# A linear-attention block and a multiplicative FFN on one core: the last 882 of 1382 steps in another order

## The chip, the cores and the metric

The kernel runs on one core of a Trainium2 chip. The metric is the device time of one execution in microseconds. Of the kernel before there are three runs, 556.48, 558.15 and 558.35 us, with a median of 558.15.

The engines are named as in the profile: PE (TensorE's matmuls), PEld (its weight loads), DVE (VectorE), ACT (ScalarE), POOL (GpSimd) and SP (SyncE, which issues the DMAs here).

## The reference

```python
# deltanet, q k v: (4, 8, 768, 48), beta: (4, 8, 768)
k_n = k / (np.linalg.norm(k, axis=-1, keepdims=True) + 1e-06)
for t in range(S):
    y[:, :, t] = np.einsum('bhd,bhde->bhe', q[:, :, t], state)
    v_old = np.einsum('bhde,bhd->bhe', state, kt)
    state = state + bt[:, :, :, None] * np.einsum('bhd,bhe->bhde', kt, vt - v_old)
# bridge: (B,H,S,D) -> (B*S, H*D), x is 3072 x 384
# ffn, w1 w2: (384, 1024), w3: (1024, 1024), w_out: (1024, 384)
a = x @ w1
b = x @ w2
h = a * b @ w3
return (h @ w_out).astype(np.float32)
```

All values are float32.

## The kernel before

**The attention.** The 768 positions are cut into 12 chunks of 64, two of which make a pair. Within a chunk the recurrence is solved in closed form: a triangular matrix U of scaled key scores is inverted, and the state passes from chunk to chunk. For one chunk m, the steps and their lines are these.

- d: the keys and queries are transposed on DVE into KQ (L355).
- s: the scores, in two halves. PE writes one PSUM buffer of the pool "ps_w" (L451, L457), DVE makes U (L463) and the masked query scores PT (L474) out of it. The pool has two buffers, used in turn by everything that writes ps_w.
- u and V: U of a pair goes out to DRAM and comes back in blocks of 32 (DMAs Ud<-U L491, Ub<-Ud L510). DVE inverts the blocks in place, 31 pairs of operations on Vb (L524, L529). Then Vb goes out (L549) and comes back as T and TT.
- e: the corner between the blocks, with two bursts of small matmuls (L619) and a copy on ACT behind each (L635, L646).
- c: the chain. PE multiplies S and KQ (L672), DVE makes the right-hand side R (L706), PE multiplies R and TT, DVE makes X (L717), PE multiplies X and the keys, and DVE makes the next state S (L738). Each needs the one ahead of it.
- y: the outputs (L777), which are three bursts on PE, first KQ and S, then PT and X, then KQ and S again. ACT copies them into xT (L795), and DMAs move some strips of xT (L806).
- g, N and n are the keys' norms (POOL's squares L301, DVE's sums L303, small DVE operations L310 to L334) and the scaling of v on POOL (L658). k, v and p are loads.

**The FFN.** Behind a pair u stand the FFN's 256 positions of each batch pair. The step a makes ab = (x w1) * (x w2) in eight pieces: PE (L934), a copy by ACT (L946), PE again (L934), and DVE's multiply out of PSUM (L950). S is sums of these pieces on POOL (L1007). o multiplies by the folded w3 w_out in seven products of 16 matmuls (L1166, a fast matrix multiplication with seven products instead of eight). x adds the products up on DVE and ACT (L1197, L1201, L1203) and stores them (L1182). PE's results of the FFN lie in the pool "ps_f" with four banks, used in turn. The last pair has another form of a (L1074) with sums made on POOL (X and W, L1026 to L1052).

**The order.** Each step is a piece of a generator. ORDER (L39 to L87) is a string of 1382 step names, and each name advances one generator by one piece. A name whose generator has ended does nothing. At the end every engine's instructions are bound to the order in which they were written:

```python
    for name in ORDER.split():
        step(name)
    in_text_order()
```

So ORDER sets the order on each engine, and an engine that waits for one instruction holds up all that stand behind it. It also sets which buffer of a pool a step gets, since pools are used in turn. The text overlaps three things: while the blocks of one pair are inverted on DVE, PE runs the products a of an earlier pair, and in between PE mixes the products o with the short bursts of s, e, c and y.

## Time and profile before

| what | us |
|---|---|
| median of three runs | 558.15 |
| lowest, highest | 556.48, 558.35 |
| span of the profiled execution | 556.1 |
| PE busy in it | 533.6 |
| DVE busy | 343.7 |
| ACT busy | 145.7 |
| POOL busy | 169.7 |

The profiled execution's own time is not listed apart from its span. The median of the runs lies 2.05 us above that span. In the rows that the prediction quotes, times are microseconds, the first number of a timeline row is its start within the span, the second its duration, and brackets hold the idle time of that engine just before, with what ended it. The steps that are moved begin at about 152 us.

### The profile page before, as it was taken

How to read it: one execution, taken by the hardware profiler on the slowest of the kernel's cores; microseconds unless marked ns; L12 is line 12 of the kernel's file. 1: busy time of each engine (PE TensorE's matmuls, PEld its weight loads, DVE VectorE, ACT ScalarE, POOL GpSimd, SP SyncE). 2: the span in 40 equal slices, each digit the busy share in tenths (PEclk: the TensorE clock that was granted, in tenths of full speed). 3: DMA queues.
4: the chain of work that ended last, by engine and by line, in shares of the span. 5: the costliest groups of instructions: out<-in, count | busy, mean ns of one | idle time of the engine just before them, and what ended most of it. 6: DMA issues, size and time to landing. Idle time of an engine off the chain costs nothing.

```text
span 556.1 us, 19932 instructions
## 1 busy us (share of the span) xinstructions
PE 533.6 (96%) x8732; PEld 390.8 (70%) x8732; DVE 343.7 (62%) x800; ACT 145.7 (26%) x291; POOL 169.7 (31%) x213
## 2 busy tenths in 40 slices
PE   6699999999999999999999999999999999989997
PEld 5556667788998544888444897445995447988897
DVE  6799738589546498574995354885373973213552
ACT  2786567531121120220111211202201102212200
POOL 7574443527730002812102522004540027420000
PEclk9999999999999999999999999999999999999999
DMA  9999956594423593453745453605307222020001
GB/s 189 339 307 230 158 140 150 128 160 55 96 48 55 119 147 72 67 88 89 122 74 100 70 91 80 126 38 83 51 15 154 26 60 38 18 58 1 0 2 57
DMA packets 191527, 54.22 MB, mean 98 GB/s; under 512 B 178928, under 2 KB 185072, under 8 KB 191440
## 3 DMA queue, kind: packets, MB, share of 16 engines
q1 hardware_dynamic: 189328, 52.56, 46.3%
q8 instruction: 68, 1.11, 0.9%
q10 hardware_dynamic: 2112, 0.39, 0.5%
q14 instruction: 19, 0.16, 0.1%
HBM read 41.78 MB, written 9.96 MB: 93 GB/s over the span
## 4 chain that ended last, share of the span: by engine, by line
PE 93%; DVE 3%; issue 2%; DMA 2%; ACT 0%; SPq 0%; DVEq 0%
PE ps_f L934 38%; PE ps_f L1166 20%; PE ps_f L913 7%; PE ps_w L672 6%; PE ps_w L777 4%; PE ps_f L1074 4%; PE ps_w L619 3%; PE ps_w L1074 2%; PE ps_w L451 2%; PE ps_f L369 1%; PE ps_w L457 1%; PE ps_f L904 1%; DMA beta_fm<-in_beta_dram 1%; PE ps_w L409 1%; PE ps_w L1166 1%
## 5 line engine op out<-in xcount | busy, mean ns | idle before, releaser
L934 PE MATMUL ps_f<-xT,w2s 128*128 128x512 f32 (+1 forms) x288 | 106.9, 524 | 0.0
L934 PE MATMUL ps_f<-xT,w1s 128*128 128x512 f32 (+1 forms) x288 | 106.7, 524 | 0.0
L934 PEld LDWEIGHTS ps_f<-xT,w2s 128*128 128x128 f32 x288 | 54.1, 190 | 46.5 <-issue 41.6
L934 PEld LDWEIGHTS ps_f<-xT,w1s 128*128 128x128 f32 x288 | 54.0, 190 | 45.3 <-issue 41.6
L1007 POOL TENSOR_TENSOR ab<-ab 128x256 f32<-128x256 f32 x80 | 56.4, 731 | 78.7 <-DVE ab L950 73.8
L946 ACT COPY ab<-ps_f 128x512 f32<-128x512 f32 (+1 forms) x48 | 24.3, 515 | 134.4 <-PE ps_f L934 130.3
L1166 PE MATMUL ps_f<-w,ab 128*128 128x192 f32 x320 | 57.3, 332 | 1.9 <-DVE osb L1197 1.3
L1166 PEld LDWEIGHTS ps_f<-w,ab 128*128 128x128 f32 x320 | 51.6, 190 | 3.3 <-issue 2.4
L524 DVE TENSOR_TENSOR tb<-Vb,Ub 128x31 f32<-128x31 f32 (+15 forms) x124 | 43.0, 347 | 15.4 <-DMA Ub<-Ud 11.5
L529 DVE TENSOR_TENSOR Vb<-Vb,tb 128x31 f32<-128x31 f32 (+15 forms) x124 | 43.0, 346 | 4.3
L913 PE MATMUL ps_f<-wo,w3T 128*128 128x384 f32 x128 | 43.5, 491 | 0.4 <-ACT w3T L907 0.4
L1166 PE MATMUL ps_f<-room,ab 128*128 128x192 f32 x240 | 42.8, 332 | 0.0
L950 DVE TENSOR_TENSOR ab<-ab,ps_f 128x512 f32<-128x512 f32 (+1 forms) x48 | 27.4, 589 | 24.0 <-PE ps_f L934 24.0
L1166 PEld LDWEIGHTS ps_f<-room,ab 128*128 128x128 f32 x240 | 38.7, 190 | 0.7
L913 PEld LDWEIGHTS ps_f<-wo,w3T 128*128 128x128 f32 x128 | 23.5, 190 | 15.4 <-ACT w3T L907 0.5
L301 POOL TENSOR_TENSOR sq<-ktok 128x384 f32<-128x384 f32 x24 | 19.7, 835 | 43.5 <-DMA out_dram<-osb 16.9
L658 POOL TENSOR_TENSOR vtok<-vtok,n 128x384 f32<-128x384 f32 x24 | 19.8, 832 | 39.5 <-DMA vtok<-in_v_dram 39.5
L635 ACT COPY T<-ps_w 32x512 f32<-32x512 f32 x24 | 13.8, 577 | 67.2 <-PE ps_w L619 46.2
L795 ACT COPY xT<-ps_w 112x256 f32<-112x256 f32 x48 | 14.3, 384 | 65.0 <-PE ps_w L777 61.7
L451 PE MATMUL ps_w<-KQ 48*64 48x128 f32 x320 | 21.9, 274 | 1.8 <-DVE PT L474 1.5
L717 DVE TENSOR_TENSOR X<-ps_w,wt 128x768 f32<-128x768 f32 x12 | 11.5, 956 | 19.4 <-PE ps_w L672 12.9
L1197 DVE TENSOR_TENSOR room<-room,ps_f 128x384 f32<-128x384 f32 (+1 forms) x13 | 7.0, 537 | 26.4 <-PE ps_f L1166 26.4
(170 smaller groups left out, 805.9 us busy)
## 6 DMA issues: line engine op xcount, KB each, us to landing
vtok<-in_v_dram SPq DMA_DIRECT2D x24, 192.0 KB, 4.4
out_dram<-osb SPq DMA_DIRECT2D x23, 192.0 KB, 2.6
ktok<-in_k_dram SPq DMA_DIRECT2D x44, 96.0 KB, 3.4
raw<-in_moe_w_dram SPq DMA_DIRECT2D x8, 512.0 KB, 6.2
raw<-in_moe_w_dram SPq DMA_DIRECT2D x18, 192.0 KB, 4.5
raw<-in_moe_w_out_dram SPq DMA_DIRECT2D x7, 384.0 KB, 5.3
Ud<-U SPq DMA_DIRECT2D x40, 64.0 KB, 2.8
Ub<-Ud SPq DMA_DIRECT2D x5, 512.0 KB, 4.2
```

The costliest lines, as they stand in the source:

```text
L451: pe.matmul(ps[half(z), 0, n : n + 128], lhsT=x[:, 0, :], rhs=x.rearrange("p j t -> p (j t)"), start=True, stop=True,)
L524: dve.tensor_tensor(out=tv, in0=V[:, 0 : s + 1, s : s + 1].to_broadcast([P, s + 1, n]), in1=U[:, s, s + 1 : BS].unsqueeze(1).to_broadcast( ...
L529: dve.tensor_tensor(out=o, in0=o, in1=tv, op=ALU.subtract)
L672: pe.matmul(out(ps, r, h, z), lhsT=lhs(r, h, z), rhs=rhs(r, h, z), start=True, stop=True,)
L777: i = pe.matmul(region(h, z, r), lhsT=lhs, rhs=rhs, start=part[n] not in part[:n], stop=part[n] not in part[n + 1 :],)
L913: pe.matmul(ps[:, 0:DM], lhsT=w3Ts[jc, kc // 4][:, kc % 4 * P : kc % 4 * P + P], rhs=wo(kc), start=(kc == 0), stop=(kc == KF - 1),)
L934: pe.matmul(ps[:].rearrange("p b c t -> p b (c t)"), lhsT=w[:, m, js], rhs=x[:, m, :, c0:c1].rearrange("p b c t -> p b (c t)"), start=(m = ...
L946: act.copy(out=t, in_=ps)
L950: dve.tensor_tensor(out=t, in0=t, in1=ps, op=ALU.mult)
L1007: (dve if u == last else pool).tensor_tensor(out=o_, in0=x_, in1=y_, op=op)
L1074: pe.matmul(ps[:, j, :], lhsT=w[j], rhs=x, start=first and j == 0, stop=j == 1, skip_group_check=not first,)
L1166: pe.matmul(ps[b][:, b, :], lhsT=ab_of(u, HF * f + i, t0), rhs=ws_[w][:, i], start=first and i == 0 and (b == 0 or n == "F"), stop=i == HF ...
```

## The change

ORDER is replaced. The first 500 names are the same, the other 882 are the same names in another order, and nothing is added or removed. One more line is needed for the string, so every line number behind it is higher by one in the changed kernel. The words with the change say that VectorE's SBUF-only operations are kept off GpSimd's. The core of the diff is one line of the table before, and the one in which the same steps stand now:

```diff
-o0 x0 y3 s4 s4 d5 d5 s4 s4 N2 s5 y3 u4 s5 V2 s5 s5 s5 N2 s5 c3 u5 V2 x0 p6 x0 a14 p6 a14 a14 a14
...
+c3 c3 S0 o0 S0 S0 S0 S0 x0 x0 x0 c3 c3 y3 y3 d5 d5 s4 s4 s4 s4 d5 d5 y3 s4 s4 s5 s5 s5 u4 s5 s5
```

The following rows show three places. The first is the run of chunks 3 to 5, ahead of the first inversion that is moved. PE's order there, before, from the chain of chunk 3 to the scores of chunk 4 ("R,TT" is the chain's multiplication, "room" and "w" are weights of the products o):

```order
L672 MATMUL ps_w<-R,TT_89 64x48 x32
L1166 MATMUL ps_f<-room,ab 128x192 x8
L777 MATMUL ps_w<-KQ,S 48x64 x16
L777 MATMUL ps_w<-PT,X 48x64 x32
L777 MATMUL ps_w<-KQ,S 48x64 x16
L451 MATMUL ps_w<-KQ 64x128 x2
```

And PE's order there in the changed kernel:

```order
L673 MATMUL ps_w<-R,TT_89 64x48 x32
L778 MATMUL ps_w<-KQ,S 48x64 x16
L778 MATMUL ps_w<-PT,X 48x64 x32
L778 MATMUL ps_w<-KQ,S 48x64 x16
L452 MATMUL ps_w<-KQ 64x128 x2
```

The product o has left its place between the chain and the outputs; a second one that stood between the two halves of chunk 4's scores has also gone to a place behind the scores. On DVE, the same run, before, from chunk 3's X on (kperm and qperm are the keys and queries to be transposed, osb a result to be stored; the numbers tell buffers apart, and PT_2765 and PT_2836 are chunks 4 and 5):

```order
L717 TENSOR_TENSOR X_2652<-ps_w_103,wt_1514 128x2x8x48
L1197 TENSOR_TENSOR room_2013<-room_2013,ps_f_95 128x384
L1197 TENSOR_TENSOR osb_2720<-room_2013,ps_f_93 128x384
L355 STREAM_TRANSPOSE KQ_2723<-kperm_91 128x8x64 x2
L463 TENSOR_TENSOR U_106<-ps_w_103,wt_2528 128x512
L1197 TENSOR_TENSOR osb_2759<-room_2013,ps_f_97 128x384
L474 TENSOR_TENSOR PT_2765<-ps_w_103,smask_86 128x512
L355 STREAM_TRANSPOSE KQ_2723<-qperm_92 128x8x64 x2
L463 TENSOR_TENSOR U_106<-ps_w_101,wt_2528 128x512
L474 TENSOR_TENSOR PT_2765<-ps_w_101,smask_86 128x512
```

The same in the changed kernel, where PT_2758 and PT_2819 are chunks 4 and 5:

```order
L718 TENSOR_TENSOR X_2659<-ps_w_103,wt_1514 128x2x8x48
L356 STREAM_TRANSPOSE KQ_2730<-kperm_91 128x8x64 x2
L464 TENSOR_TENSOR U_106<-ps_w_103,wt_2413 128x512
L475 TENSOR_TENSOR PT_2758<-ps_w_103,smask_86 128x512
L356 STREAM_TRANSPOSE KQ_2730<-qperm_92 128x8x64 x2
L464 TENSOR_TENSOR U_106<-ps_w_101,wt_2413 128x512
L475 TENSOR_TENSOR PT_2758<-ps_w_101,smask_86 128x512
```

DVE's own list is the same but for the additions to osb, which have moved away; chunk 5's query transposes still stand behind chunk 4's first U and PT.

The second place is the end of the mixed part. PE's order before, from the chain of chunk 11 to the last stage's first features (L1074):

```order
L672 MATMUL ps_w<-R,TT_89 64x48 x32
L1166 MATMUL ps_f<-room,ab 128x192 x8
L777 MATMUL ps_w<-KQ,S 48x64 x16
L777 MATMUL ps_w<-PT,X 48x64 x32
L777 MATMUL ps_w<-KQ,S 48x64 x16
L1166 MATMUL ps_f<-room,ab 128x192 x8
L1166 MATMUL ps_f<-w_117,ab 128x192 x8
L1074 MATMUL ps_f<-xT,w1s 128x256 x6
```

And in the changed kernel:

```order
L673 MATMUL ps_w<-R,TT_89 64x48 x32
L778 MATMUL ps_w<-KQ,S 48x64 x16
L778 MATMUL ps_w<-PT,X 48x64 x32
L778 MATMUL ps_w<-KQ,S 48x64 x16
L1167 MATMUL ps_f<-room,ab 128x192 x16
L1075 MATMUL ps_f<-xT,w1s 128x256 x2
L1167 MATMUL ps_f<-w_117,ab 128x192 x8
```

Here too the product between chain and outputs has gone behind the outputs, and two features of the last stage now stand ahead of the last product of the pair before.

The third place is the first moved inversion. DVE's order before, at its end:

```order
L524 TENSOR_TENSOR tb_3062<-Vb_2833,Ub_2902 128x31
L529 TENSOR_TENSOR Vb_2833<-Vb_2833,tb_3062 128x31
L950 TENSOR_TENSOR ab_2992<-ab_2992,ps_f_93 128x512
L355 STREAM_TRANSPOSE KQ_3081<-kperm_91 128x8x64 x2
L355 STREAM_TRANSPOSE KQ_3081<-qperm_92 128x8x64
L950 TENSOR_TENSOR ab_3074<-ab_3074,ps_f_95 128x512
```

In the changed kernel, inside the inversion, behind 22 of its 31 pairs:

```order
L525 TENSOR_TENSOR tb_3006<-Vb_2237,Ub_2896 128x220
L530 TENSOR_TENSOR Vb_2237<-Vb_2237,tb_3006 128x22x10
L951 TENSOR_TENSOR ab_2989<-ab_2989,ps_f_97 128x512
L525 TENSOR_TENSOR tb_3018<-Vb_2237,Ub_2896 128x207
L530 TENSOR_TENSOR Vb_2237<-Vb_2237,tb_3018 128x23x9
```

Before, the stage's first multiply stands ahead of the 31 pairs and the second behind them all. Now the first stands behind 22 pairs, and the rest behind all of them.

## The prediction

> **What bounds the kernel now.** I read the page first: the busy shares, then the chain that ended last.

> ```profile
> PE 533.6 (96%) x8732; PEld 390.8 (70%) x8732; DVE 343.7 (62%) x800; ACT 145.7 (26%) x291; POOL 169.7 (31%) x213
> PE 93%; DVE 3%; issue 2%; DMA 2%; ACT 0%; SPq 0%; DVEq 0%
> ```

> TensorE (PE) is busy 96% of the span and 93% of the last chain. VectorE (DVE) is 3% of that chain. A reordering that removes no work can therefore win only idle time of PE, or lose by adding some. The second view is the busy time by stretch, cut where the stages change. Its columns are the stretch, its length, busy time and instructions of PE, PEld, DVE, ACT and POOL, the granted clock, the DMA share and GB/s.

> ```profile
> 152.00:265.00 113.00, 109.64 (x2408) 80.66 (x2408) 72.81 (x173) 18.97 (x41) 25.04 (x36) 1.00 0.48 86
> 265.00:303.00 38.00, 38.00 (x216) 17.60 (x211) 30.60 (x76) 4.70 (x9) 4.91 (x6) 1.00 0.58 98
> 342.00:381.00 39.00, 39.00 (x266) 18.20 (x256) 29.35 (x77) 4.80 (x9) 3.12 (x5) 1.00 0.43 91
> ```

> The kernel alternates. In 265 to 303 and 342 to 381, where DVE inverts the triangular blocks and PE runs the first two products of the FFN, PE is busy all of the time. In the stretches between, where scores, state and outputs go back and forth between PE and DVE, it idles a little. The clock is 1.00 in every row, so no term comes from it. The third view sums what PE waited for from 152 us on, which is where the changed steps begin. Its columns are the total, the number of waits and the longest.

> ```profile
> PE ps_f L1166 <- DVE osb L1197: 1.3, 1, 1.3
> PE ps_w L451 <- DVE PT L474: 1.0, 3, 0.5
> PE ps_w L672 <- issue: 0.8, 2, 0.5
> PE ps_w L672 <- DVE X L717: 0.5, 1, 0.5
> PE ps_f L1166 <- DVE tb L524: 0.5, 1, 0.5
> PE ps_w L672 <- DVE PT L474: 0.2, 1, 0.2
> ```

> That is 4.3 us, of which 0.8 us ("issue") waits for nothing that the order names. So 3.5 us in seven waits is what an order could remove.

> **What the change removes.** The lengths of single waits come from PE's timeline: start, duration, what ran, and in brackets the idle time before it.

> ```profile
> 156.43 0.77 PE L619 MATMUL ps_w<-T,U 33*33 33x32 f32 x64
> 157.69 0.94 PE L672 MATMUL ps_w<-X,ktok 64*48 64x48 f32 x64 [0.49 <-DVE X L717]
> 162.32 0.77 PE L619 MATMUL ps_w<-T,T 33*33 33x32 f32 x64
> 163.01 2.87 PE L1166 MATMUL ps_f<-room,ab 128*128 128x192 f32 x16
> ```

> A burst of 64 corner matmuls hands over to the next 0.69 us after its start (162.32 to 163.01). At 156.43 the next burst started 1.26 us after, so the wait cost 0.57 us against the 0.49 that stands as idle, because the modelled end of a burst overlaps its successor. With 0.08 us more for each, the seven waits are worth 3.5 + 7 x 0.08 = 4.1 us. In the new order each of their places is arranged otherwise, and I count all of it as removed.

> The change also leaves fewer entries into the large matmuls. Counted in PE's order from the first changed row on, there are 40 uninterrupted runs of large matmuls before and 36 after.

> ```profile
> 152.73 2.80 PE ps_f L1166 x16
> 534.35 13.00 PE ps_f L1166 x80
> ```

> In the chain, 16 such matmuls entered from small ones take 2.80 us, and in a run of 80 they take 13.00 / 5 = 2.60 us. An entry costs 0.2 us, and four fewer give 0.8 us.

> **What the name of the change says.** It keeps DVE's operations on SBUF away from GpSimd's (POOL). The trace shows what that is worth:

> ```profile
> 269.88 0.40 DVE L524 TENSOR_TENSOR tb<-Vb,Ub 128x231 f32<-128x231 f32 x1
> 270.01 0.95 POOL L301 TENSOR_TENSOR sq<-ktok 128x384 f32<-128x384 f32 x1 [16.94 <-DMA out_dram<-osb]
> 270.31 0.90 DVE L529 TENSOR_TENSOR Vb<-Vb,tb 128x231 f32<-128x231 f32 x1
> 274.40 0.42 DVE L529 TENSOR_TENSOR Vb<-Vb,tb 128x255 f32<-128x255 f32 x1
> 274.84 0.83 POOL L301 TENSOR_TENSOR sq<-ktok 128x384 f32<-128x384 f32 x1 [3.88 <-DVE Vb L529]
> 274.86 1.09 DVE L524 TENSOR_TENSOR tb<-Vb,Ub 128x256 f32<-128x256 f32 x1
> ```

> Beside a POOL square the two DVE operations take 0.90 and 1.09 us where their neighbours take 0.40 and 0.42, so 0.50 + 0.67 = 1.2 us are lost. Both lie inside 265 to 303, where PE is busy 38.00 of 38.00 us. DVE has slack there (30.60 of 38.00), so the loss reaches nobody. I put this relief at 0. Its bounds are 0 and 1.2 us.

> [...]

> **What the change adds.** In each mixed stretch I read the new order of PE and DVE row by row, asking how much PE work stands between a burst and the DVE result that the following one needs. The prices come from these rows:

> ```profile
> 156.68 0.96 DVE L717 TENSOR_TENSOR X<-ps_w,wt 128x768 f32<-128x768 f32 x1 [2.48 <-PE ps_w L672]
> 174.71 0.27 PE L451 MATMUL ps_w<-KQ 48*64 48x128 f32 x1
> 174.95 1.19 ACT L795 COPY xT<-ps_w 112x256 f32<-112x256 f32 x4 [5.54 <-PE ps_w L777]
> 175.75 2.87 PE L1166 MATMUL ps_f<-w,ab 128*128 128x192 f32 x16
> 175.88 0.69 DVE L463 TENSOR_TENSOR U<-ps_w,wt 128x512 f32<-128x512 f32 x1 [0.86 <-PE ps_w L457]
> 180.45 0.68 DVE L474 TENSOR_TENSOR PT<-ps_w,smask 128x512 f32<-128x512 f32 x1
> 177.55 1.29 DVE L355 STREAM_TRANSPOSE KQ<-qperm 128x512 f32<-128x512 f32 x2
> 486.99 0.67 PE L777 MATMUL ps_w<-KQ,S 48*48 48x64 f32 x32
> 487.47 1.08 PE L777 MATMUL ps_w<-PT,X 64*48 64x64 f32 x64
> ```

> *Chunks 3 to 5 (near 165 to 182 us).* Before, a product of 2.80 us stands between R,TT and the outputs, and hides X. Now the outputs follow R,TT directly. X is ready 1.26 us after the point where PE could go on (the row at 157.69), and KQ,S covers 0.48 (486.99 to 487.47): 0.8 us of wait. Chunk 4's second half of the scores now follows its first half directly. It needs the bank that ACT empties at 174.95 + 1.19 = 176.14, while the first half ends at 175.75: 0.4 us. Chunk 5's scores need the query transposes. These now stand on DVE behind U and PT: 0.13 (175.75 to 175.88) + 0.6 + 0.6 + 1.29 = 2.6 us after the first half. The 0.4 us wait and the second half itself (1.0 us, as 174.71 to 175.75) cover 1.4 of that, so 1.2 us are left. Two smaller waits behind PT follow in the same run, 0.2 us each. Together 2.8 us, of which the first 0.8 is as good as certain.

> *Chunks 5 to 7.* Half a score burst's bank is free about 1.5 us after its burst (0.13 + 0.6 + 0.68, and a start), and a state burst covers 1.0 of it. This stands twice: 0.5 + 0.5. A tenth comes from c5's short chain. The last product of the pair still follows the one that DVE's x1 must free a bank for, as before at 0.5 us. Together 1.6 us.

> *Chunks 9 and 10.* S,KQ to R,TT needs 1.26 us, and half a score burst of about 1.0 lies between: 0.3. The next half waits for PT behind R: 0.6. Together 0.9 us.

> *Chunks 10 and 11 (the end).* Chunk 11 has the same R,TT, KQ,S, PT,X as above: 0.8. The corner's copy on ACT stands between e10 and c10: 0.5. Then the first matmuls of the last stage stand ahead of the last product, and need the xT transfers:

> ```profile
> 490.61 3.74 SPq L806 DMA_DIRECT2D xT<-xT  x6
> 495.90 2.34 POOL L1052 TENSOR_TENSOR xT<-xT 128x256 f32<-128x256 f32 x3 [16.81 <-DMA xT<-xT]
> ```

> The transfers are issued until 494.35, and POOL reads xT at 495.90. Two products after the outputs end about 494.7. The wait is between 0 and 1.2 us, and I take 0.3, since the first matmuls need only the earlier strips. It replaces the 1.3 us for osb in the waits above. Together 1.6 us.

> **The sum.** 2.8 + 1.6 + 0.9 + 1.6 = 6.9 us added, 4.1 + 0.8 = 4.9 removed: 2.0 us more. The profiled span is 556.1 us, and the median of the runs, 558.15, lies 2.05 above it, which I leave as it is. So 556.1 + 2.0 + 2.05 = 560.2 us. If 3 us of the unsure waits are covered, 3.9 us are added, and the time is 557.2. If each of ten waits is 0.3 us longer than its row, it is 563.2.

> **The inversions.** The four later inversions hold the rest of the change. There PE now does more of the w1 products first, and DVE's multiplies stand elsewhere among the inversion's steps.

> ```profile
> 181.09 5.49 SPq L491 DMA_DIRECT2D Ud<-U  x8
> 188.13 0.34 SPq L510 DMA_DIRECT2D Ub<-Ud  x1
> 188.52 0.95 SPq L1182 DMA_DIRECT2D out_dram<-osb  x1
> 192.96 0.19 DVE L524 TENSOR_TENSOR tb<-Vb,Ub 128x31 f32<-128x31 f32 x1 [3.51 <-DMA Ub<-Ud]
> 216.21 0.68 DVE L950 TENSOR_TENSOR ab<-ab,ps_f 128x512 f32<-128x512 f32 x1
> 183.31 39.05 PE ps_f L934 x90
> ```

> A product of six matmuls takes 39.05 / 15 = 2.6 us, and an inversion takes 23.3 us (192.96 to 216.21). Counting products until the first bank that must be freed by DVE, I find at least 0 to 0.7 us of slack in the second inversion, 0.3 in the fourth, 2.3 in the first, and more in the third. On SP's queue, a store and two loads of v now stand between Ud and Ub in the first one: 0.95 + 2 x 0.6 (5.49 / 8 each) = 2.2 us of issue, of which the 1.55 us gap (186.58 to 188.13) hides most. 0.6 us later costs nothing against 2.3. I put the inversions at 0.

> **The rivals.** *Covered waits.* The bursts on PE arrive later than I count, and DVE and ACT are earlier. Then only what is removed counts, with the certain 0.8 twice: 558.15 - 4.9 + 1.6 = 554.9. For it speaks that most of DVE's and ACT's work in these stretches is short. Against it, the rows at 156.68 and 175.88 start at once behind PE, so DVE is not late and cannot become earlier. If the 1.2 us of the two long rows came off as well, it would be 553.7.

> *The banks.* An inversion that starts late keeps the multiplies queued behind its steps, and PE's product waits for a bank. It decides from 0.3 us late in the fourth and 0.7 in the second. If Ub lands 3 us later in each, which nearly doubles the 3.51 us that DVE waits for it at 192.96, PE loses 0.7 + 2.6 + 2.7 = 6 us on top: about 566, slower than before by more than 1%. For it speaks the number of transfers now between Ud and Ub; against it, PE's row of 38.00 in 38.00.

> *The change does nothing.* The loss that it names is 1.2 us off PE's path, and added and removed waits cancel: 558.2.

> **Chances.** The forecast, 557 to 563, has 0.60; covered waits 0.15; the banks 0.17; nothing 0.08. The measurement of this kernel can tell about 0.5%, or 2.8 us. Faster by more than that (under 555.4) is two thirds of the covered waits: 0.10. Slower (over 560.9) is the banks and a third of the forecast: 0.37. The same is left with 0.53. The range is 555.5 to 564.0: it leaves out most of the first rival's gain and the upper half of the second's.

> **What would show it.** Right: in the waits after, DVE's X ahead of PT,X (L778) twice at 0.7 to 0.9 us; KQ's transposes (L356) ahead of L452 at about 1.2; the 1.3 us osb wait gone; PE's sum of idle from 152 us on at 6 to 8 us; the stretch of each inversion still full. Whether inversion steps still take 0.9 us beside POOL changes nothing. Wrong: idle under 4 us in all, or a wait of L935 for DVE's multiply (L951).

## The result and the profile after

| | us |
|---|---|
| before, median of 6 runs | 557.76 (556.48 to 558.53) |
| after, median of 6 runs | 565.13 (561.47 to 567.03) |
| after, the profiled execution | 566.52, span 564.8 |

The ratio after to before is 1.0132, with an interval of 1.0108 to 1.0156. The changed kernel is 7.4 us slower. The prediction said 560.2, with a range from 555.5 to 564.0, and the measured time lies 1.1 us above the range. Its sign is right, and its size is 4.9 us too small. A second set of the same kernel on another chip had a median of 563.36 (run 10 below). The ratios come with a 95% interval and are not quotients of the medians shown; one execution, the slowest of s2's four, is left out of them.

The page of the kernel after shows the engines' busy time and the last chain.

```profile
PE 535.5 (95%) x8732; PEld 392.2 (69%) x8732; DVE 347.4 (62%) x800; ACT 145.9 (26%) x291; POOL 169.3 (30%) x213
PE 73%; DVE 13%; DMA 5%; issue 4%; SPq 4%; ACT 1%; POOL 0%; ACTq 0%; DVEq 0%; POOLq 0%
```

PE has the same 8732 matmuls and 1.9 us more busy time. What grew most is its idle time, from 22.5 to 29.3 us of the span. The chain has changed more than the time did: it now leaves PE for an inversion on DVE, for DMA and for SP. The stretches that the prediction quoted read as follows.

```profile
152.00:265.00 113.00, 108.23 (x2327) 78.94 (x2314) 72.13 (x168) 18.89 (x41) 23.01 (x33) 1.00 0.47 83
265.00:303.00 38.00, 38.00 (x157) 17.75 (x156) 28.96 (x70) 5.85 (x10) 3.95 (x5) 1.00 0.68 116
342.00:381.00 39.00, 39.00 (x221) 18.74 (x220) 27.86 (x74) 4.50 (x8) 2.53 (x4) 1.00 0.60 116
```

The inversions still lie under a full PE, 38.00 of 38.00 and 39.00 of 39.00 us. The mixed stretch has 1.4 us more idle time. PE's largest waits from 152 us on, and two smaller ones that the prediction named, are these.

```profile
PE ps_w L620 <- DVE T L603: 2.3, 1, 2.3
PE ps_w L778 <- DVE X L718: 1.4, 2, 0.7
PE ps_w L673 <- issue: 1.1, 2, 0.9
PE ps_w L778 <- issue: 1.0, 2, 0.7
PE ps_f L1167 <- DVE room L1198: 0.7, 1, 0.7
...
PE ps_w L452 <- ACT xT L796: 0.4, 1, 0.4
...
PE ps_w L452 <- DVE KQ L356: 0.2, 1, 0.2
```

X stands twice at 0.7, as predicted. KQ is 0.2 where 1.2 was expected. At the head stands a wait that no step of the prediction has: the corner's burst L620 waits 2.3 us for T. Two "issue" rows, 2.1 us together, wait for nothing that the order names. Before, there were 0.8 us of these. All waits from 152 us on add up to 10.3 us, where the prediction had named 6 to 8 as a sign of being right. The 1.3 us wait for osb is gone. A wait of L935 for L951, which it had named as a sign of being wrong, is there with 0.3 us.

**Where it went.** To keep the modelled ends out of the sum, I measure from the start of each matmul to the start of the next and take off the usual distance of that shape. Of what is left from 152 us on, gaps over 0.16 us are single waits, and the rest is entries into large matmuls and rounding.

| from 152 us on | before | after |
|---|---|---|
| single gaps over 0.16 us | 10.1 | 18.4 |
| of these, stalls inside bursts ("issue") | 1.2 | 3.0 |
| of these, the corner that waits for T | 0 | 2.5 |
| slower matmuls in 3.4 us of half clock | 0 | 1.7 |
| the small rest | 21.9 | 21.2 |

Added up, the kernel after has 18.4 - 10.1 + 1.7 - 0.7 = 9.3 us more, against 8.7 us between the spans. Three entries have no term in the prediction: packets of instructions 1.8, the corner 2.5, the clock 1.7, in all 6.0 us. The waits that it did sum make up the other 3.3, where it had 2.0. All of this is one execution of each kernel.

**The corner.** SP's timeline of the kernel before, around the inversion of chunks 8 and 9:

```profile
345.30 0.34 SPq L510 DMA_DIRECT2D Ub<-Ud  x1
372.12 0.35 SPq L549 DMA_DIRECT2D Vd<-Vb  x1
374.81 1.91 SPq L583 DMA_DIRECT2D TT<-Vd  x4
...
378.78 2.05 SPq L583 DMA_DIRECT2D TT<-Vd  x4
```

The same of the kernel after:

```profile
347.23 0.53 SPq L511 DMA_DIRECT2D Ub<-Ud  x1
378.00 0.36 SPq L550 DMA_DIRECT2D Vd<-Vb  x1
382.99 1.91 SPq L584 DMA_DIRECT2D TT<-Vd  x4
...
387.00 4.96 SPq L262 DMA_DIRECT2D qperm<-in_q_dram  x8
392.01 2.12 SPq L584 DMA_DIRECT2D TT<-Vd  x4
```

The first row is 1.9 us later, and from there to Vd it takes 30.8 us instead of 26.8: DVE starts on Ub 5.67 instead of 3.44 us after its issue, and the steps, with more of DVE's other work among them, take 25.1 instead of 23.3 us. From Vd to the first TT it takes 5.0 instead of 2.7 us. Then the loads of a later chunk's queries hold SP for 4.96 us, and only after them come the other four TT. In all they start 13.2 us later (378.78 to 392.01). DVE and PE of the kernel after show who waits for it:

```profile
352.90 0.19 DVE L525 TENSOR_TENSOR tb<-Vb,Ub 128x31 f32<-128x31 f32 x1 [6.58 <-DMA Ub<-Ud]
395.89 0.71 DVE L603 STREAM_TRANSPOSE T<-TT 128x512 f32<-128x512 f32 x1 [4.68 <-DMA TT<-Vd]
```

```profile
391.48 2.87 PE L1167 MATMUL ps_f<-room,ab 128*128 128x192 f32 x16
396.65 0.76 PE L620 MATMUL ps_w<-T,U 33*33 33x32 f32 x64 [2.31 <-DVE T L603]
```

DVE waited 6.58 us for Ub and 4.68 for TT, and PE 2.31 for T.

**The clock.** The two stretches of 2 us behind that wait, in the kernel after:

```profile
396.00:398.00 2.00, 1.35 (x68) 1.31 (x69) 1.18 (x3) 0.55 (x1) 1.07 (x2) 0.98 0.28 49
398.00:400.00 2.00, 2.00 (x8) 2.00 (x7) 0.00 (x0) 0.61 (x2) 0.00 (x0) 0.50 0.00 0
```

The granted clock is 0.50 for 3.41 us (397.93 to 401.34 in the trace). A product of 16 takes 4.55 us there instead of 2.87.

**The packets.** PE's timeline of the kernel after shows one burst of 64 that stops 6 matmuls ahead of its end:

```profile
251.95 1.14 PE L673 MATMUL ps_w<-R,TT 64*64 64x48 f32 x58 [0.18 <-DVE R L707]
254.03 0.33 PE L673 MATMUL ps_w<-R,TT 64*64 64x48 f32 x6 [0.94 <-issue]
```

No operand is missing there, since the six need what the 58 needed. The page's queue of instructions suggests why it stops there:

```profile
q8 instruction: 68, 1.11, 0.9%
```

These are 68 packets and 1.11 MB, so 16.4 KB each (16,384 bytes in the trace). PE's records in the trace are 8732 matmuls, 8732 weight loads and 122 others (semaphores and drains), 17,586 in all. That is 68.7 times 256, so that a packet would carry 256 of PE's instructions, 64 bytes each. The four stalls inside bursts stand at the records 8897 (250.27 us), 9153 (254.03), 13761 (410.21) and 16833 (494.38), and from each to the next the count is a multiple of 256. Whether the packets make these stalls is tested below (d1 to s4).

### The profile page after: what moved, and what is told of

It reads as the page before. It is cut to its first block, busy times and chain, and to the rows that moved or that the text cites. A ratio compares the mean times of both kernels' runs of the same rounds, so it can differ in the third digit from the quotient of the medians.

```text
span 564.8 us, 19930 instructions
## 1 busy us (share of the span) xinstructions
PE 535.5 (95%) x8732; PEld 392.2 (69%) x8732; DVE 347.4 (62%) x800; ACT 145.9 (26%) x291; POOL 169.3 (30%) x213
## 3 DMA queue, kind: packets, MB, share of 16 engines
q8 instruction: 68, 1.11, 0.9%
## 4 chain that ended last, share of the span: by engine, by line
PE 73%; DVE 13%; DMA 5%; issue 4%; SPq 4%; ACT 1%; POOL 0%; ACTq 0%; DVEq 0%; POOLq 0%
PE ps_f L935 23%; PE ps_f L1167 18%; PE ps_f L914 7%; PE ps_w L673 5%; PE ps_w L778 4%; PE ps_f L1075 4%; DVE tb L525 4%; DVE Vb L530 3%; PE ps_w L620 3%; PE ps_w L1075 2%; DMA Ub<-Ud 2%; PE ps_w L452 1%; PE ps_f L370 1%; SPq L492 1%; DMA ktok<-in_k_dram 1%
## 5 line engine op out<-in xcount | busy, mean ns | idle before, releaser
L935 PE MATMUL ps_f<-xT,w2s 128*128 128x512 f32 (+1 forms) x288 | 107.0, 524 | 0.3 <-DVE ab L951 0.3
L935 PE MATMUL ps_f<-xT,w1s 128*128 128x512 f32 (+1 forms) x288 | 106.0, 522 | 0.0
L935 PEld LDWEIGHTS ps_f<-xT,w1s 128*128 128x128 f32 x288 | 54.4, 190 | 46.0 <-issue 42.6
L935 PEld LDWEIGHTS ps_f<-xT,w2s 128*128 128x128 f32 x288 | 54.1, 190 | 46.4 <-issue 41.9
L1167 PE MATMUL ps_f<-w,ab 128*128 128x192 f32 x320 | 58.7, 338 | 0.9 <-DVE tb L525 0.5
L1167 PEld LDWEIGHTS ps_f<-w,ab 128*128 128x128 f32 x320 | 53.3, 195 | 2.7 <-issue 1.0
L525 DVE TENSOR_TENSOR tb<-Vb,Ub 128x31 f32<-128x31 f32 (+15 forms) x124 | 42.7, 345 | 19.1 <-DMA Ub<-Ud 15.3
L951 DVE TENSOR_TENSOR ab<-ab,ps_f 128x512 f32<-128x512 f32 (+1 forms) x48 | 27.6, 591 | 30.6 <-PE ps_f L935 30.6
L452 PE MATMUL ps_w<-KQ 48*64 48x128 f32 x320 | 22.5, 275 | 2.6 <-issue 0.9
L718 DVE TENSOR_TENSOR X<-ps_w,wt 128x768 f32<-128x768 f32 x12 | 11.4, 954 | 19.5 <-ACT TT L647 6.6
L525 DVE TENSOR_TENSOR tb<-ps_w,Ub 128x31 f32<-128x31 f32 (+15 forms) x62 | 21.0, 339 | 3.2 <-DMA Ub<-Ud 1.8
```

Source lines behind the costliest of these rows:

```text
L452: pe.matmul(ps[half(z), 0, n : n + 128], lhsT=x[:, 0, :], rhs=x.rearrange("p j t -> p (j t)"), start=True, stop=True,)
L525: dve.tensor_tensor(out=tv, in0=V[:, 0 : s + 1, s : s + 1].to_broadcast([P, s + 1, n]), in1=U[:, s, s + 1 : BS].unsqueeze(1).to_broadcast( ...
L935: pe.matmul(ps[:].rearrange("p b c t -> p b (c t)"), lhsT=w[:, m, js], rhs=x[:, m, :, c0:c1].rearrange("p b c t -> p b (c t)"), start=(m = ...
L951: dve.tensor_tensor(out=t, in0=t, in1=ps, op=ALU.mult)
L1167: pe.matmul(ps[b][:, b, :], lhsT=ab_of(u, HF * f + i, t0), rhs=ws_[w][:, i], start=first and i == 0 and (b == 0 or n == "F"), stop=i == HF ...
```

## The experiments

Each run is compared with runs of the kernel before on the same chip. Steps are named as in the order's string.

**1. The corner's loads behind the corner (e1).** The changed kernel, one step moved:

```diff
-e8 e8 a37 p11 N4 e8 e8
+e8 e8 a37 N4 e8 e8
...
-e8 o3 e9 e9 e9
+e8 o3 e9 p11 e9 e9
```

> The changed kernel (565.1 us median, 1.0132 of before), with one name moved: the eight loads of the queries (second piece of p11) stand behind the loads for chunk 9's corner (first piece of e9) on SP's queue instead of ahead of them. Theory A, the corner's late loads: TT of chunk 9 is issued at about 387 instead of 392 us, DVE's transpose (L603) is done before PE gets there, PE's 2.3 us wait at L620 and the half-clock stretch behind it (about 2 us) go: 560 to 562 us, ratio 1.005 to 1.009, granted clock 1.00 from 152 us on. Rival B, the loss is the sum of the many small waits that the prediction counted, and the lower clock is chance: no more than the 2.3 us go and the clock still falls in some runs, 563 to 565 us, ratio 1.010 to 1.014.

Measured: 565.98 us (562.74 to 567.58), ratio 1.0148 (1.0104 to 1.0192). The wait for T has left the profile, and the time has not moved. Rival B's 563 to 565 us is nearer than theory A's 560 to 562. PE's timeline shows what has grown instead:

```profile
409.28 0.32 PE L778 MATMUL ps_w<-KQ,S 48*48 48x64 f32 x6 [1.27 <-issue]
409.53 4.55 PE L1167 MATMUL ps_f<-room,ab 128*128 128x192 f32 x16
```

A burst stops six matmuls before its end, and the product behind it takes 4.55 us, as at the granted clock of 0.50 above, instead of 2.87. The changed kernel has the same stall at 410.21 us, with 0.96 us from start to start; here it is 1.48. PE's order is the same in both, and yet the stalls inside bursts add up to 4.0 us here and 3.0 there. So the corner alone does not explain the loss, and why the stalls grew is not shown.

**2. The same wait put into the kernel before (e2).**

```diff
-V4 V4 e8 a31 d10 a31
+V4 V4 e8 p11 a31 d10 a31
...
-e9 e9 e9 p11 e9 c8 a32
+e9 e9 e9 e9 c8 a32
```

> The kernel before (557.8 us), with one name moved: the eight loads of the keys for chunk 11 (first piece of p11) stand ahead of the loads for chunk 9's corner on SP's queue, as the loads of the queries do in the changed kernel. Chunk 9's transpose, now at 384.4 us, comes about 5 us later, and PE's row at 387.0 waits for it. Theory A: a new wait of PE of 2 to 3 us at L619 near 387 us, perhaps with a stretch of half clock: 560 to 562 us, ratio 1.004 to 1.008. Rival B, PE has enough other work there: 557.8 us, ratio 1.000.

Measured: 559.49 us (558.15 to 563.91), ratio 1.0045 (1.0017 to 1.0073), before 557.25. The row in PE's timeline:

```profile
387.82 0.76 PE L619 MATMUL ps_w<-T,U 33*33 33x32 f32 x64 [2.30 <-DVE T L602]
```

The median is 2.2 us higher, and the interval puts the cost between 0.9 and 4.1 us. This corner is a real cost, and here the order of the loads on SP makes it. The same wait did not bring a half clock in this execution:

```profile
386.00:388.00 2.00, 0.18 (x20) 0.18 (x23) 0.94 (x2) 0.00 (x0) 0.00 (x0) 1.00 0.59 94
388.00:390.00 2.00, 2.00 (x130) 1.95 (x121) 1.42 (x4) 1.15 (x2) 1.12 (x2) 1.00 0.14 25
```

The three slowest of its nine executions (560.61, 561.74 and 563.91) are those with a mean granted clock of 0.994 to 0.997; no other has a value between 0.988 and 0.999. Of the 18 executions of the kernel before on this chip one has such a value (0.997), and it is the slowest, 560.19.

**3. The products put back between chain and outputs (e3).** In the changed kernel, o0 stands between c3 and y3 again, and products stand between c11 and y11:

```diff
-x0 c3 c3 y3 y3 d5
+x0 c3 c3 o0 y3 y3 d5
...
-v4 x0 V2 o0 x0 V2 a15
+v4 x0 V2 x0 V2 a15
...
-c10 c10 c10 o4 x4 y10 n11 y10
+c10 c10 c10 y10 n11 y10
...
-c11 c11 o4 S4 S4 c11 c11 y11
+c11 c11 o4 x4 S4 S4 c11 c11 o4 y11
```

> The changed kernel, with a product of 16 matmuls put back between the chain's R,TT and the outputs of chunks 3 and 11 (o0 behind c3; o4's third and fourth a place later). It leaves the corner of chunk 9 as it is. Theory A (the prediction's own terms are right at these two places, and small): the two waits of L778 for X, 0.70 us each, go and nothing else: 1.4 us less, 563.7 us, ratio 1.0105. Rival B, the small waits are the main loss and hang together: 3 us or more less, under 562 us, ratio under 1.0075. Rival C, the wait only moves to the next small burst: 565 us, ratio 1.013.

Measured: 569.03 us (566.37 to 571.33), ratio 1.0208 (1.0166 to 1.0251). The waits for X are gone, and the kernel is slower than the changed one. PE's waits show what came for them:

```profile
PE ps_w L778 <- issue: 2.2, 2, 1.2
PE ps_w L673 <- issue: 1.7, 2, 1.3
PE ps_f L935 <- DVE osb L1198: 1.6, 1, 1.6
PE ps_w L620 <- DVE T L603: 1.4, 1, 1.4
PE ps_w L452 <- DVE KQ L356: 1.2, 2, 1.1
```

"Issue" has doubled, from 2.1 to 4.3 us with a row not shown (0.4), and nothing that the edit moves is what these bursts wait for. The KQ wait of 1.1 us is the one that the prediction had expected of the change itself.

**4. The contention taken away (e5).** In the kernel before, the two squares that ran beside DVE's long rows are made by ACT:

```diff
-                pool.tensor_tensor(out=sq[:], in0=kt[:, r], in1=kt[:, r], op=ALU.mult)
+                if j == 4 and cc + r == 1:
+                    act.activation(out=sq[:], in_=kt[:, r], func=ACTF.Square)
+                else:
+                    pool.tensor_tensor(out=sq[:], in0=kt[:, r], in1=kt[:, r], op=ALU.mult)
```

> The kernel before, with two of POOL's 24 squares made by ACT instead, which are the two that lay beside inversion steps at 270 and 275 us. The two inversion steps of 0.90 and 1.09 us then take 0.40 to 0.43, and that inversion ends 1.2 us earlier on DVE. Theory A, this contention lies off PE's path: no change, 557.8 us, ratio 1.000 (within 0.15%). Rival B, it is on the path: 556.6 us, ratio 0.998.

Measured: 557.71 us, ratio 1.001 (0.9995 to 1.0025). The two DVE rows are 0.40 and 0.42 us now:

```profile
270.61 0.40 DVE L532 TENSOR_TENSOR Vb<-Vb,tb 128x231 f32<-128x231 f32 x1
274.66 0.42 DVE L527 TENSOR_TENSOR tb<-Vb,Ub 128x256 f32<-128x256 f32 x1
```

The contention that the change's name speaks of was real, 1.2 us of DVE's time, and PE gains nothing when it goes.

**5 and 6. Halves of the two orders (h1, h2).** h1 has the changed order to the fifteenth step of V4 and the remaining steps in the old order from there, h2 the reverse. The seam of h1 against the changed order, and then that of h2 against the old one:

```diff
-V4 V4 V4 V4 V4 V4
+V4 V4 V4 Q3 v9 K2 N4 c7 c7 a32 a32 N4 k10 a30
...
-V4 V4 V4 V4 a35 a37 V4 V4 V4 k11 a34 n9
+V4 V4 V4 K0 Q2 K1 Q0 K3 p10 x2 k11 p11 d10
```

> The order of the changed kernel up to the middle of the inversion of chunks 8 and 9 (its 15th step), and the order of the kernel before for all that is left. PE's gaps in the profiles, start to start, give the stages apart: up to there the changed kernel has 2.7 us more than the kernel before, 4.1 us and a half-clock stretch of 1.7 us in the stage behind it, and 1.5 us in the last one. Theory A, the stages add up: 559 to 561 us, ratio 1.003 to 1.007. Rival B, the first stages cost nothing and all comes with the late corner of chunk 9: 557 to 558 us, ratio under 1.002.

> The other way about: the order of the kernel before up to the 15th step of the inversion of chunks 8 and 9, and the order of the changed kernel for what is left. Theory A: the late corner (less late, since that inversion starts as before), the last stage's 1.5 us and some half-clock stretches: 560 to 563 us, ratio 1.004 to 1.010. Rival B: 557 to 559 us, the loss is all in the earlier part.

Measured: h1 573.54 us, ratio 1.0297 (1.0275 to 1.0318); h2 562.16 us (561.09 to 565.43), ratio 1.0115 (1.0077 to 1.0153). A row of h1 shows that the seam (the place where the two orders meet) made a wait of its own:

```profile
364.69 7.64 PE L935 MATMUL ps_f<-xT,w1s 128*128 128x512 f32 x11 [9.04 <-DVE wt L293]
```

No conclusion can be drawn from h1. In h2, whose first half is the old one, 5.2 us of loss (562.16 - 556.96) come with the second half; 1.4 of them are a wait for a bank near 375 us, which neither whole order has at that place. h2's profiled execution (561.20) has no half clock behind 26.6 us.

**7, 8 and 9. More small matmuls (d1, d2, d3).** If PE outruns its instructions, more small matmuls at one place must bring a stall there. The kernel before, with a burst repeated whose results are the same each time:

```diff
-        def products(out, lhs, rhs):
+        def products(out, lhs, rhs, n=1):
...
-            for r in range(NR):
+            for r in [r for i in range(n) for r in range(NR)]:
...
-                by_tokens_of_features, lambda r, h, z: KQ[feat(h % 2), NR * z + r, h // 2, 0, :], state
+                by_tokens_of_features, lambda r, h, z: KQ[feat(h % 2), NR * z + r, h // 2, 0, :], state,
+                3 if c == 4 else 1,
```

d1 is this, chunk 4's S,KQ three times, which adds 128 matmuls and 128 weight loads, exactly one packet. d2 has chunk 5's R,TT three times instead. d3 has S,KQ twice, half a packet.

> The kernel before, with the burst of 64 small matmuls S,KQ of chunk 4 (near 222 us, just behind 90 large matmuls) issued three times; the two repeats write the same values again. 128 matmuls and their weight loads are 256 instructions, which is one 16 KB packet of PE's instruction transfers in the profile. Theory S, a stretch of small matmuls outruns these packets: here the packets are ahead, so the repeats cost their own time, 2 x 0.97 = 1.9 us, and no new issue wait, 559.5 us, ratio 1.003. Rival T, issue waits come from elsewhere: the same 1.9 us.

> The kernel before, with the burst of 64 small matmuls R,TT of chunk 5 (near 250 us, behind 192 small matmuls of the scores) issued three times, writing the same values again. Theory S: the packets come no faster than one in 3.4 to 3.6 us, so the repeats cost 3.4 to 3.6 us instead of 1.9, and the issue wait near 251 us grows from 0.5 to 2 us or more: 561 us, ratio 1.006, and a half-clock stretch in some runs. Rival T: 1.9 us as in the other run, the issue wait stays at 0.5, 559.5 us, ratio 1.003.

> The kernel before with chunk 4's burst S,KQ issued twice instead of three times, so that 192 small matmuls follow one another there and not 256. If about two packets, 512 instructions or 256 matmuls with their weight loads, are ahead after a stretch of large matmuls (theory S as the run with three shows it, where the wait came after 246), there is no issue wait here: 0.97 us on top, 558 us, ratio 1.0015 to 1.0025, no half clock. Rival V, every repeat costs issue time in proportion: an issue wait of 0.8 us, 559 us, ratio 1.003 to 1.004.

Measured: d1 561.83 us, ratio 1.0092 (1.0062 to 1.0122). d2 563.05 us, ratio 1.0108 (1.0089 to 1.0128). d3 564.38 us, ratio 1.012 (1.0087 to 1.0152). In d1's timeline of PE the stall stands right behind the added burst:

```profile
225.77 0.26 PE L619 MATMUL ps_w<-T,U 33*33 33x32 f32 x9
227.50 1.01 PE L619 MATMUL ps_w<-T,U 33*33 33x32 f32 x55 [1.48 <-issue]
```

Theory S, by which packets are ahead behind large matmuls, expected no stall in d1, and there is one of 1.48 us. In d2 it expected the stall near 251 us to grow to 2 us or more, and it is 1.92 there. d3 adds half of d1's work and costs no less (564.38 against 561.83 us, with the kernel before at 557.05 and 556.96; the intervals overlap). As expected it has no stall at the added burst, but its time was to be 558 us. It has moved every later boundary by half a packet, and its waits from 152 us on show it:

```profile
PE ps_w L672 <- issue: 3.2, 4, 1.2
PE ps_w L778 <- issue: 2.3, 2, 1.2
...
PE ps_w L619 <- issue: 1.3, 1, 1.3
```

That is 6.8 us of "issue" in seven waits, where the kernel before has 0.8. The last is over 260 us behind the edit.

**10. The changed kernel again (a2).** No edit.

> The changed kernel once more, beside the next ones on the same chip: 564 to 566 us, ratio 1.011 to 1.016. In its profile, issue waits of about 3 us in the middle of bursts, near 250, 253, 409 and 494 us, and the wait for chunk 9's corner.

Measured: 563.36 us (560.76 to 564.1), ratio 1.0094 (1.0063 to 1.0126). The profiled execution is the fastest of the four, 560.76. It has no half clock behind 26 us, and its corner starts without a wait:

```profile
389.46 2.87 PE L1167 MATMUL ps_f<-room,ab 128*128 128x192 f32 x16
392.34 0.76 PE L620 MATMUL ps_w<-T,U 33*33 33x32 f32 x64
```

The waits for X (1.4) and "issue" (2.0) are there as ever. So in these two traces the corner and the clock come and go, and the others stay. From Vd's issue to the first TT it takes 2.85 us here (375.51 to 378.36) and 4.99 in the trace of the kernel after, which is most of the difference at the corner. The clock is not the main loss: four of the ten executions of the changed kernel have a mean granted clock of 1.00, and they took 560.76 to 564.10 us.

**11 and 12. Spacers against the waits (r1, r2).** The changed kernel with products moved to where PE waits; r1 has e1's move of p11 too:

```diff
+c3 c3 y3 o0 y3 d5
...
-y4 y4 o1 e5 e5 p7
+y4 y4 e5 e5 o1 p7
...
-S4 c11 c11 y11
+S4 c11 c11 S4 S4 o4 y11
```

> The changed kernel with three products put between bursts of small matmuls (o0's seventh behind the outputs of chunk 3 instead of behind the scores of chunk 5, o1's fourth behind the corner's second burst of chunk 5 instead of ahead of it, o4's fifth ahead of the outputs of chunk 11), and the loads for chunk 9's corner ahead of the queries' loads. Theory S, long runs of small matmuls outrun the instruction packets and the DVE results: about 2.5 us of gaps go in the first of these places and the second, 1.5 in the third, up to 2.5 at the corner, and with them most half-clock stretches: 558 to 561 us, ratio 1.002 to 1.007. Rival T, the gaps only move: 563 us or more, ratio over 1.011.

> As the run before, but without the move of the corner's loads. Theory S: 1 to 4 us above that run, 560 to 563 us, ratio 1.006 to 1.011. Rival U, the corner's wait is taken up by another wait when it goes, as it was in the first run of that move: no difference to the run before.

Measured: r1 566.5 us, ratio 1.0158 (1.0116 to 1.0199); r2 567.55 us, ratio 1.0177 (1.0156 to 1.0198). The changed kernel took 563.36 on this chip (a2), so neither gains anything, and r2 is slower. Theory S had put them at 558 to 561 and 560 to 563 us. r2 is 1.05 us above r1, with intervals that overlap, so what the move of p11 is worth here is not decided. The end of r1 shows where the product that had been pulled forward is now missing:

```profile
502.43 1.10 PE L1075 MATMUL ps_f<-xT,w1s 128*128 128x256 f32 x4 [2.48 <-DMA xT<-xT]
```

The last stage's first features now reach PE before xT has landed. It is the same term that the prediction had put between 0 and 1.2 us, and without its cover it is 2.48.

**13 to 16. The boundaries alone (s1 to s4).** The changed kernel with 32, 64, 96 and 128 more matmuls in chunk 1's S,KQ, long before the first moved step. So the order behind is kept, and the boundaries shift by 0.25, 0.5, 0.75 and a whole packet. The edit of s1:

```diff
-        def products(out, lhs, rhs):
+        def products(out, lhs, rhs, extra=0):
...
-            for r in range(NR):
+            for r in [i % NR for i in range(extra + NR)]:
...
-                by_tokens_of_features, lambda r, h, z: KQ[feat(h % 2), NR * z + r, h // 2, 0, :], state
+                by_tokens_of_features, lambda r, h, z: KQ[feat(h % 2), NR * z + r, h // 2, 0, :], state,
+                1 if c == 1 else 0,
```

> The changed kernel with 32 more small matmuls (64 instructions, weight loads counted) in chunk 1's S,KQ, long before the first moved step: the same order behind it, but every boundary of 256 instructions falls 64 instructions earlier. The profile of the changed kernel gives the time between the shifted boundaries; each pair nearer than 3.6 us is taken to stall PE for what is missing. By that count its own boundaries from 152 us on would cost 7.0 us (3.0 were found), the shifted ones 10.1. Theory K (where the boundaries fall sets a good part of the time): 565.1 + 0.5 for the matmuls + 3 = 568.6, with new stalls near 162 (1.6), 316 (1.5), 417 (1.3) and 470 us (1.6) of the old kernel's time. Theory L (a stall at a boundary only takes the place of a wait that would come anyway): 565.6.

> The same with 64 more small matmuls (128 instructions, half a packet). The count of boundaries nearer than 3.6 us gives 14.7 us. Theory K: 565.1 + 1.0 + 7.7 = 573.8, at the least 571, and the dearest of the four; new stalls near 162 (1.5), 248 (1.2), 315 (1.9), 334 (1.4), 470 (1.6), 485 us (1.5). Theory L: 566.1.

> The same with 96 more small matmuls (192 instructions). The count gives 10.7 us. Theory K: 565.1 + 1.5 + 3.7 = 570.3, less than with 64 more; new stalls near 311 (1.8), 413 (1.0), 469 (1.4), 484 us (1.5). Theory L: 566.6.

> The same with 128 more small matmuls (256 instructions, a whole packet): the boundaries of all moved steps are again where they are in the changed kernel. Theory K: 565.1 + 2.0 = 567.1, the same stalls as the changed kernel behind 152 us, and less than with 64 or 96 more although it has more work. Theory L: 567.1 too, but above the three others.

| | added packet | median us | ratio to before (interval) | stalls at boundaries, 26 to 152 us | from 152 us on |
|---|---|---|---|---|---|
| after | 0 | 565.13 | 1.0132 (1.0108 to 1.0156) | 1.1 | 3.0 |
| s1 | 0.25 | 585.44 | 1.0495 (1.045 to 1.0539) | 5.0 | 9.5 |
| s2 | 0.5 | 582.84 | 1.0362 (1.0295 to 1.043) | 7.0 | 11.4 |
| s3 | 0.75 | 575.97 | 1.0316 (1.028 to 1.0351) | 7.5 | 3.8 |
| s4 | 1 | 571.55 | 1.0223 (1.0174 to 1.0272) | 3.4 | 2.8 |

The kernel before took 559.03 us on this chip. The time rises with a quarter of a packet and falls from there while the work still grows. The kernels s1 and s4 differ by 96 matmuls in chunk 1 and behind them only in where the boundaries lie. These are their "issue" waits from 152 us on, s1 first:

```profile
PE ps_w L779 <- issue: 3.8, 3, 1.9
PE ps_w L673 <- issue: 3.0, 3, 1.3
...
PE ps_w L620 <- issue: 1.2, 1, 1.2
```

```profile
PE ps_w L779 <- issue: 1.5, 2, 1.1
...
PE ps_w L673 <- issue: 0.7, 1, 0.7
```

That is 8.0 against 2.2 us, and the control with a whole packet has the stalls of the changed kernel from 152 us on. Theory L, by which a stall only takes the place of another wait, would have given 566 us for s1 and is out by 19. Theory K is right in the cause and wrong in sizes: it had 568.6 for s1 and 573.8 for s2 as the dearest, where they took 585.4 and 582.8. Two things are missing in it. The stalls ahead of 152 us move as well, to 5.0 us in s1 (2.5 at 88 and again at 102 us) and 7.5 in s3 (3.85 of them at 102.6) from 1.1 in the kernel after. And half-clock stretches come with stalls: in s1's profile (mean granted clock 0.985) 10.2 us at 0.50 begin at 100.9, inside that second stall, and two more stretches follow. s4's profiled execution, without such stretches behind its first 26 us (mean 0.988), took 567.07, as K had it; its other three took 571 to 573, at a mean granted clock of 0.985 to 0.994, so that the control gives the stalls back and not the whole time.

## Why the prediction was wrong, by its steps

**Right: what bounds the kernel.** The sum of PE's idle time decided, the matmuls did not change, and the contention was worth nothing to PE (e5). The change did not even remove it: the inversions' steps L524 and L529 went from 43.0 + 43.0 to 42.7 + 43.0 us, and beside two of POOL's squares at 287.49 us the steps of 128x87 take 0.76 and 0.75 us in the kernel after, where at 353.86 and 354.14 they take 0.25. The four fewer entries were put at 0.8 us, and the small rest, which also holds rounding, fell by 0.7.

**Right: the waits for X.** They were put at 0.8 twice. Measured from start to start, they are 0.91 and 0.90. The bank behind ACT's xT was put at 0.4; it is 0.38 in the waits and 0.59 from start to start. Chunks 9 and 10 were put at 0.3 + 0.6 and measure 0.39 + 0.62.

**Too large: the KQ transposes.** They were put at 1.2 and measure 0.2 in the waits, 0.42 from start to start. The row of 1.1 in e3, where the wait for X ahead of it is gone, shows that the mechanism is real. In the changed kernel the waits ahead of it, for X and for ACT, let DVE catch up. I added waits that stand in a row as if each began on time.

**Too small: the small terms.** Places that I had at 0 to 0.5 us, or did not have, hold 0.4 to 0.9 each: a bank at 217 us 0.42, the wait for ss at 223 us 0.48, and at the end the wait for room 0.90 and the one ahead of the last product 0.62. The seven old waits were too small as well: from start to start they are 4.9 us, where I had 4.1. All in all the summed terms were 3.3 us net, where I had 2.0.

**The step that failed: "I put the inversions at 0".** It is the largest of three terms that I put at nothing; "issue" and the clock, below, are the other two. I asked only whether PE would run out of banks while an inversion ran. It didn't: the rival of the banks is 0.3 us in the waits after. That its time, about 566, lies nearer to the measured one than my forecast is luck. But an inversion also has a result. Its way goes from Ud over Ub, 62 operations on DVE and Vd to TT and T, and everything on SP's queue between these stands in that way. I priced the transfers ahead of Ub in the first inversion and not the query loads between the two TT groups of the third. e2 shows the price in the kernel before: a wait of 2.30 and a median 2.2 us higher. In the changed kernel it is paid in some executions (2.31, and none in a2). In these two traces that goes with the time from Vd's issue to the first TT, 4.99 and 2.85 us. a2's span of 559.0 us, with neither the corner nor a half clock, is only 2.9 above the kernel before. That is near the 2.0 of the sum, in part by luck, since its "issue" is 2.0 us where the kernel before has 0.8.

**The term that had no place: "issue".** The prediction's own table held 0.8 us of it, and I set it aside as something that no order could remove. A new order does not remove the boundaries, but it decides which matmuls fall between two of them. They cost 1.2 us before and 3.0 after in the profiles. s1 to s3 show that their place, with the half clocks that follow, moves the time by more than the whole change did.

**"The clock is 1.00 in every row, so no term comes from it."** This read the kernel before and took it for a property of the work. In the kernel after, 3.41 us at 0.50 follow the corner's 2.31 us of idle time, and they cost 1.7 us. That the idle time alone decides it is not so: e2 has the same wait, 2.30 us, and no half clock in its profile (mean granted clock 1.00), and a2 has neither.

**The repairs.** e1 took the corner away, e3 the X waits, r1 the corner and one of the X waits, r2 that wait alone, and none gained: stalls at the boundaries grew (e1, e3), or another wait was uncovered (r1, r2). No version here is faster than the kernel before. How much of each single execution's time goes to corner, clock and packets stays open, since only one execution of each set has a trace. No shift that was tried helps the changed kernel: three of the four made it much slower, and the fourth brings the stalls behind 152 us back to what they were. Four positions do not rule out a better one.

## What to carry to other kernels

When PE runs bursts of small matmuls, count its instructions as well as its waits: here, each "issue" wait of over half a microsecond inside a burst was a packet boundary, and an edit ahead that changes the count moves all the later ones. For a step that makes data for a later stage, follow its result over every queue to whoever reads it; a full PE above it says only that it does not hurt while it runs. And where single repairs only move the idle time about, as they did here, a price list of the old order's waits can be too low for a new one.

## What the runs showed of the hardware

**The granted clock falls to half for 3.41 us at a time.** Behind the first 26 us it fell to 0.50 for 3.41 us or a multiple of it (6.83 in d1, 10.24 in s1). The falls came behind 2.31 us of idle time with a burst of small matmuls (the kernel after) and behind a stall of 1.27 us (e1), and in d1 inside a stall of 1.48 us. One in e1 (at 178.35) came among several waits of under 1 us each. The idle time does not decide it alone: 2.30 us in e2 brought no fall (1.00 from 386 to 390 us). What else decides it is not shown. Between the first and the last change of the clock, each stretch at one clock is a whole multiple of 3.413 us in all profiles: the one of the kernel before is 156 of them, those of the kernel after are 1, 4, 109, 1 and 48, and those of e1 1, 67, 1 and 45.
